# A two-dimensional spectral filter beside a token MLP: the second transform split by two instead of by four, with the combining step moved behind its matmuls

## The chip, the core and the metric

The kernel runs on one core of one Trainium2 chip. The metric is device time in microseconds (us) of one execution, median of several. Five engines work side by side, each through its own list of instructions in order: TensorE (PE in the profile; PEld are its weight loads), VectorE (DVE), ScalarE (ACT), GpSimd (POOL, nearly unused here) and SyncE (SP), which issues the DMA transfers. TensorE writes into the accumulator memory (PSUM); VectorE and ScalarE take results out of it.

## The reference

Two branches read the same x, 2048 rows (tokens) of 512 values in bf16, and a gate per row mixes them.

```python
g = sigmoid((x * gate_w).sum(-1, keepdims=True))
X = rfft2(x, axes=(-2, -1)) * (w_r + 1j * w_i)      # 2048 x 257 complex
a = irfft2(X, s=(2048, 512)).astype(bfloat16)
h = layernorm(x)
u = gelu(einsum("bsd,sf->bdf", h, w1) + b1)         # F = 1792
b = (einsum("bdf,fs->bds", u, w2) + b2).transpose(0, 2, 1)
out = g * a + (1 - g) * b
```

The first branch is a Fourier transform over rows (length 2048) and over columns (length 512), a product with a table of complex weights, and the inverse. The second is a layer norm and an MLP that mixes rows.

## The kernel before

**The MLP** is 448 accumulating matmuls' worth of 512 columns: `m1` (line 684 of the profile, 224 matmuls into 14 accumulators, gelu by ScalarE at 700) and `m2` (line 983, the same number of products, taken out by ScalarE at 989, the last two of the sixteen output tiles by VectorE at 1001). It needs nothing of the spectral branch until the very end, so its matmuls fill whatever time TensorE would wait for that branch.

**The spectral branch** is done as small transforms by matmul with radix steps by additions on VectorE between them. The names in the code, in order:

- Row index s = 512q + 4p + r. For each r (0 to 3), `q4a`/`q4b` (519 to 526) do the radix 4 over q; then `fa` (538 to 541) transforms over p by matmul. The weights (the stationary operand) of these matmuls are 128 columns of x, so the result has a column index d on the partitions: four blocks `dq` of 128 consecutive d. ScalarE evicts each into `X` (544).
- `d4a`/`d4b` (551 to 558) do the first radix 4 of the column transform, over the four blocks, on VectorE, for each r.
- `radix4(..., inverse=False)` (577 to 590) combines the four r. It runs for two halves of the frequencies, `lt` = 1 and then `lt` = 0, each as e1 (two instructions of 2048 elements per partition), e2 and e3 (two of 1024 each). The zeroth line is special: `sp0`/`sp1` (602 to 620) work on it apart, and line 628 copies it into `X` for `lt` = 0.
- `fb` (646 to 649) is the second transform: over the 128 d of a block, by matmul, for each `lt`, each of four `e` and real and imaginary part `c`: 16 groups of four matmuls. Two have 128 output columns; the other two, for the odd frequency classes, have 256 and add up in place. `fbev` (653, ScalarE) evicts each group into `B`; the accumulator holds the frequencies by class b (f = b + 4i), and the eviction reads them in turn from the four classes, so that `B` is in order of f.
- `c0a` (770, 771) copies the column of frequency 0, `nyq` (780 to 783) treats one further row, `bfly` (799, 800), `mul` (807), `comb` (812, 813), `ob` (819 to 821) form the product with the complex weights `W`, all on VectorE, first for `lt` = 0, then 1. `wprep` (756 to 760) and `c0b` prepare it.
- The inverse: `radix4(..., inverse=True)` on `B` (577, 578, 582, 583, 592, 593), whose results `T` the first inverse matmuls `i1` (868 to 875) take; evictions (881, 883), additions `zf` and `fq` (891 to 904), matmuls `i3` (942 to 946), evictions with the gate as scale (955), additions `es` (966 to 970), and the sum with the MLP (995, 1001).

**What sets the order.** The kernel is written as tasks with an engine, an estimated duration, keys that they read and write, and a priority. `Plan.order` plays them through once on a model of the engines, picks on each engine the ready task of least priority value, and the tasks are then emitted in that order. So the order on every engine is fixed when the kernel is built; on the chip an instruction that waits holds up all behind it on its engine. `fa` and `fb` groups and `i1` to `i3` take accumulators of two kinds, `fa` and `fb`, two each; `m1` and `m2` mostly use four called `acc`. A priority of 2 for `fb` against 10 and more for `m1` means: as soon as the model has the operands ready, `fb` goes first.

Of the kernel before, what the change touches and what calls it, by code (L numbers as in the profile page):

```python
# [34 lines left out]
def make_tables():  # L35
# [52 lines left out]
    tb = np.zeros((P, 3, 4, 64))  # L88
    i = np.arange(64)
    for b in (0, 2):  # L90
        th = ang(p, b + 4 * i, D)
        tb[:, 0, b // 2] = np.cos(th)
        tb[:, 1, b // 2] = -np.sin(th)
    tb[:, 1, 0, 0] = alt
    tb[:, 2, 0:2] = tb[:, 0, 0:2]
    tc = np.zeros((P, 2, 3, 2, 64))
    for n, b in enumerate((1, 3)):
        th = ang(p, b + 4 * i, D)
        sg = 1.0 if b == 1 else -1.0
# [15 lines left out]
    tb = np.concatenate([tb[:, :, 0:2].reshape(P, 384), tc.reshape(P, 768), cf.reshape(P, 8)], 1)  # L115
# [152 lines left out]
def kernel(  # L268
# [137 lines left out]
    load("tb", [P, 1160], BF16, tabs["tb"], 296960, prio=9)  # L406
# [51 lines left out]


# [3 lines left out]
    for r in range(4):  # L463
# [69 lines left out]
        for dq in range(4):  # L533
            def fa(r=r, dq=dq):
                pa = t["pa", r, dq] = ps([P, 2, 2, P], F32, "fa", 2)
                ta = t["ta"][:, r, :]
                w = lambda k: t["xf", r][:, k, dq * P:(dq + 1) * P]
                T.matmul(pa[:, 1], lhsT=w(2), rhs=ta[:, 256:512], start=True, stop=False)  # L538
                T.matmul(pa[:, 1], lhsT=w(3), rhs=ta[:, 384:640], start=False, stop=True)
                T.matmul(pa[:, 0, :, 0:64], lhsT=w(0), rhs=ta[:, 0:128], start=True, stop=True)  # L540
                T.matmul(pa[:, 0, :, 64:128], lhsT=w(1), rhs=ta[:, 128:256], start=True, stop=True)  # L541
            add("PE", mm(128, 128, 256, 256), fa, reads=[("xf", r % 2), ("ta", r)], writes=[("pa", r, dq)], prio=0, alloc=["fa"],
                free=["xf"] if dq == 3 else ())
            add("ACT", act(512), lambda r=r, dq=dq: A.copy(t["X"][:, :, r, :, dq, :], t["pa", r, dq][:]),  # L544
                reads=[("pa", r, dq)], writes=[("X", r, dq)], prio=0, free=["fa"])

        def d4a(r=r):
            xv = t["X"][:, :, r]
            s = t["st"][:, 1024:2048].rearrange("p (a c n) -> p a c n", a=2, c=2)
            two = lambda lo: xv[:, :, :, lo:lo + 2, :].rearrange("p a c j l -> p a c (j l)")  # L550
            V.tensor_add(s, two(0), two(2))
            V.tensor_sub(two(2), two(0), two(2))

        def d4b(r=r):
            xv = t["X"][:, :, r]
            s = t["st"][:, 1024:2048].rearrange("p (a c n) -> p a c n", a=2, c=2)
            V.tensor_add(xv[:, :, :, 0, :], s[:, :, :, 0:P], s[:, :, :, P:2 * P])
            V.tensor_sub(xv[:, :, :, 1, :], s[:, :, :, 0:P], s[:, :, :, P:2 * P])
        add("DVE", 2 * tt(1024), d4a, reads=[], writes=[("X", r, dq) for dq in range(4)] + ["sx"], prio=3.9)
        add("DVE", 2 * tt(512), d4b, reads=["sx"], writes=[("D", r)], prio=3.9)  # L560


    def radix4(view, pq, st, pqk, stk, reads, writes, prio, inverse):
# [16 lines left out]
        def e2():  # L580
            p, q = parts(pq)
            V.tensor_add(dst(0, 1), p, q)
            V.tensor_sub(dst(4, 1), p, q)

        def e3():
            s, u = parts(st)
            sr, ur = s[:, ::-1], u[:, ::-1]
            if not inverse:
                V.tensor_add(dst(2, 5), s, ur)
                V.tensor_sub(dst(3, 3), sr, u)  # L590
            else:
                V.tensor_add(dst(3, 3), sr, u)
                V.tensor_sub(dst(2, 5), s, ur)
# [12 lines left out]
    def sp1():  # L606
        sp, sd, fx = t["sp"], t["sd"], t["fx"]
        c = 0.5 ** 0.5
        V.tensor_add(sd[:, 0], sp[:, 0:2], sp[:, 2:4])
        V.tensor_sub(sd[:, 1], sp[:, 0:2], sp[:, 2:4])  # L610
        V.tensor_add(fx[:, 0, 0], sd[:, 0, 0, 0], sd[:, 0, 1, 0])
        V.tensor_sub(fx[:, 0, 1], sd[:, 0, 0, 0], sd[:, 0, 1, 0])
        V.tensor_copy(fx[:, 1, 0], sd[:, 1, 0, 0])
        V.tensor_scalar_mul(fx[:, 1, 1], sd[:, 1, 1, 0], -1.0)
        V.tensor_scalar_mul(sd[:, 0, 0, 1], sd[:, 1, 1, 1], c)
        V.tensor_scalar_mul(sd[:, 1, 0, 1], sd[:, 0, 1, 1], -c)
        V.tensor_add(fx[:, 2, 0], sp[:, 0, 1], sd[:, 0, 0, 1])
        V.tensor_sub(fx[:, 3, 0], sp[:, 0, 1], sd[:, 0, 0, 1])
        V.tensor_sub(fx[:, 2, 1], sd[:, 1, 0, 1], sp[:, 2, 1])
        V.tensor_add(fx[:, 3, 1], sd[:, 1, 0, 1], sp[:, 2, 1])  # L620
    add("DVE", tiny(12), sp1, reads=["sp"], writes=["fx"], prio=0)

    for lt in (1, 0):
        pr = 3.0 if lt else 3.1
# [3 lines left out]
    add("DVE", 0.15, lambda: V.tensor_copy(t["X"][:, 0, :, :, :, 0], t["fx"][:]), reads=["fx"],  # L628
        writes=[("Z", 0, 0), ("Z", 0, 1)], prio=3.1)

    def tbl(kind, c):
        tb = t["tb"]
        if kind < 2:
            return tb[:, 0:384].rearrange("p (c k i) -> p c k i", c=3, k=2)[:, c:c + 2, kind, :]
        v = tb[:, 384:1152].rearrange("p (g n) -> p g n", g=2)[:, kind - 2]
        return v[:, 128 * c:128 * c + 256]

    for lt in (0, 1):
        for e in (0, 2, 1, 3):
            for c in range(2):  # L640
                tag = ("fa", "fb")[c]

                def fb(lt=lt, e=e, c=c, tag=tag):
                    pb = t["pb", lt, e, c] = ps([P, 2, 4, 64], F32, tag, 2)
                    w = lambda k: t["X"][:, lt, e, c, k, :]
                    T.matmul(pb[:, :, 0, :], lhsT=w(0), rhs=tbl(0, c), start=True, stop=True)
                    T.matmul(pb[:, :, 2, :], lhsT=w(1), rhs=tbl(1, c), start=True, stop=True)
                    for k in (2, 3):
                        T.matmul(pb[:, :, 1::2, :], lhsT=w(k), rhs=tbl(k, c), start=(k == 2), stop=(k == 3))
                add("PE", mm(128, 128, 256, 256), fb, reads=[("Z", lt, e % 2), "tb"], writes=[("pb", lt, e, c)], prio=2, alloc=[tag])  # L650

                def fbev(lt=lt, e=e, c=c):
                    A.copy(t["B"][:, lt, e, 2 * c:2 * c + 2, :].rearrange("p s (i b) -> p s i b", b=4),  # L653
                           t["pb", lt, e, c][:].rearrange("p s b i -> p s i b"))
                add("ACT", act(512), fbev, reads=[("pb", lt, e, c)], writes=[("B", lt, e)], prio=1.8, free=[tag])
# [108 lines left out]
    for lt in range(2):  # L764
# [8 lines left out]
        if lt == 0:  # L773
# [10 lines left out]
            add("DVE", 3 * d1(512) + 0.1, nyq, reads=bk + [("W", 0), ("W", 1), ("c0", 0)] + pbk, writes=["nn"], prio=0.5)  # L784
# [261 lines left out]
```

## Time and profile before

| | |
|---|---|
| median of 3 runs | 132.45 us (132.32 to 132.88) |
| the profiled execution | 132.39 us, its span 130.5 us |
| TensorE: busy, instructions | 125.4 us, 780 matmuls |
| VectorE | 110.6 us, 248 |
| ScalarE | 83.1 us, 166 |
| DMA | 23.18 MB in 17478 packets |

The span runs from the first to the last instruction of the profiled execution; the rest of its time lies around that. Instructions are listed with their start in the span, their duration, the engine, the line of the kernel, what they write and read, and, in brackets, the idle time of the engine ahead of them and what ended it. Groups ("by line") have the count, the sum of busy time, the mean in ns, and the idle time ahead. A matmul's duration is longer than the time until the next may start, since matmuls are pipelined; the step from start to start is what it costs TensorE. Likewise the durations on VectorE and ScalarE overlap a little with the next instruction's.

### The profile page before, as it was taken

What the parts mean: (1) busy time and instruction counts of PE and PEld (TensorE: products, weight loads), DVE (VectorE), ACT (ScalarE), POOL (GpSimd) and SP (SyncE); (2) the same over time, 40 slices, a digit from 0 to 9 for tenths busy, and PEclk for the clock granted to TensorE, in tenths of its full rate; (3) what the DMA queues carried; (4) which work ended last, traced back from release to release, by engine and by line L of the source; (5) the groups of instructions that cost most, each with busy time, mean ns of one, the idle gap of its engine ahead of it and who ended that gap; (6) DMA issues with size and microseconds to landing.
All of it is one profiled execution on the core that took longest, in us unless ns stands there. A gap on an engine that the chain in (4) does not pass through costs nothing.

```text
span 130.5 us, 2166 instructions
## 1 busy us (share of the span) xinstructions
PE 125.4 (96%) x780; PEld 70.7 (54%) x780; DVE 110.6 (85%) x248; ACT 83.1 (64%) x166; POOL 0.2 (0%) x4
## 2 busy tenths in 40 slices
PE   6998999999999999999999999999999999999991
PEld 2344565545544484854444555455687577655590
DVE  2689999999999997059999999999959929999961
ACT  4468989599999999996111044322499489962200
POOL 0000000000000000000000000000000000000000
PEclk9999999999999999999999999999999999999998
DMA  4999999943669536799999800000000000312331
GB/s 83 389 372 386 398 394 379 374 91 89 135 184 298 107 85 131 259 288 406 414 421 421 334 6 0 3 5 3 0 0 0 0 5 0 161 69 97 161 121 40
DMA packets 17478, 23.18 MB, mean 178 GB/s; under 512 B 1574, under 2 KB 14908, under 8 KB 17468
## 3 DMA queue, kind: packets, MB, share of 16 engines
q1 hardware_dynamic: 17180, 22.59, 50.6%
q10 hardware_dynamic: 288, 0.46, 1.3%
q8 instruction: 6, 0.10, 0.3%
q14 instruction: 4, 0.03, 0.1%
HBM read 20.93 MB, written 2.10 MB: 176 GB/s over the span
## 4 chain that ended last, share of the span: by engine, by line
PE 58%; DVE 28%; DMA 8%; issue 2%; ACT 2%; SPq 0%; DVEq 0%
PE acc L684 18%; PE acc L983 17%; DMA wa<-in_B_w_dram 5%; PE fb L684 5%; DVE xp L807 3%; DVE st L807 3%; DMA x<-in_A_x_dram 2%; PE fa L684 2%; PE fa L538 2%; DVE xp L812 2%; DVE st L578 2%; DVE B L819 2%; DVE xp L813 2%; PE fb L868 1%; PE fa L868 1%
## 5 line engine op out<-in xcount | busy, mean ns | idle before, releaser
L983 PE MATMUL acc<-gl,wb 128*128 128x512 bf16 (+1 forms) x112 | 27.4, 373 | 0.0
L983 PE MATMUL acc<-gl,wa 128*128 128x512 bf16 (+1 forms) x112 | 27.2, 372 | 0.0
L684 PE MATMUL acc<-h,wb 128*128 128x512 bf16 x112 | 25.9, 379 | 0.0
L989 ACT ACTIVATE x<-acc,ombb,omg 128x512 bf16<-128x512 f32 x14 | 10.8, 785 | 22.7 <-PE acc L983 22.7
L983 PEld LDWEIGHTS <-wb 128*128 128x128 bf16 x126 | 13.4, 114 | 10.3 <-DMA wb<-in_B_w_dram 1.2
L983 PEld LDWEIGHTS <-wa 128*128 128x128 bf16 x126 | 13.5, 114 | 9.4
L684 PE MATMUL acc<-h,wa 128*128 128x512 bf16 x64 | 17.8, 387 | 0.6 <-DVE h L505 0.6
L684 PEld LDWEIGHTS <-wb 128*128 128x128 bf16 x112 | 10.9, 98 | 11.7
L684 PEld LDWEIGHTS <-wa 128*128 128x128 bf16 x112 | 10.4, 99 | 10.8 <-issue 2.1
L700 ACT ACTIVATE gl<-acc,b1f 128x512 bf16<-128x512 f32 x11 | 7.6, 693 | 6.8 <-PE acc L684 6.8
L478 DVE BATCH_NORM_STATS2 stats<-x 128x6 f32<-128x512 bf16 x14 | 9.4, 674 | 2.2 <-DMA x<-in_A_x_dram 2.2
L544 ACT CAST X<-fa 128x512 bf16<-128x512 f32 x16 | 9.3, 582 | 2.7 <-PE fa L541 2.5
L511 ACT ACTIVATE h<-x,nmr,rstd 128x512 bf16<-128x512 bf16 x13 | 9.8, 806 | 0.4 <-DVE nmr L502 0.2
L714 ACT ACTIVATE x<-x 128x512 bf16<-128x512 bf16 x16 | 10.1, 655 | 0.0
L684 PE MATMUL fb<-h,wa 128*128 128x512 bf16 x32 | 9.4, 379 | 0.0
L955 ACT ACTIVATE B<-fb,g 128x512 bf16<-128x512 f32 x8 | 5.9, 735 | 0.0
L955 ACT ACTIVATE B<-fa,g 128x512 bf16<-128x512 f32 x8 | 5.8, 727 | 0.0
L359 PE MATMUL fa<-xp 128*128 128x512 bf16 x10 | 4.4, 632 | 1.2 <-DVE xp L320 1.2
L684 PE MATMUL fa<-h,wa 128*128 128x512 bf16 x16 | 5.6, 379 | 0.0
L653 ACT CAST B<-fb 128x512 bf16<-128x512 f32 x8 | 5.0, 628 | 0.0
L653 ACT CAST B<-fa 128x512 bf16<-128x512 f32 x8 | 4.9, 616 | 0.0
L709 DVE TENSOR_TENSOR x<-x,gw 128x2048 bf16<-128x2048 bf16 x4 | 4.8, 1216 | 0.0
(177 smaller groups left out, 230.0 us busy)
## 6 DMA issues: line engine op xcount, KB each, us to landing
wb<-in_B_w_dram SPq DMA_DIRECT2D x11, 512.0 KB
wa<-in_B_w_dram SPq DMA_DIRECT2D x7, 512.0 KB
wa<-in_B_w_dram SPq DMA_DIRECT2D x3, 896.0 KB
x<-in_A_x_dram SPq DMA_DIRECT2D x3, 512.0 KB
wb<-in_B_w_dram SPq DMA_DIRECT2D x4, 384.0 KB
out_dram<-x SPq DMA_DIRECT2D x3, 512.0 KB
rot<-dft_ti SPq DMA_DIRECT2D x1, 736.5 KB
rot<-dft_ta SPq DMA_DIRECT2D x4, 160.0 KB
```

The source lines that it names most:

```text
L478: V.bn_stats(out=t["stats"][:, j, :], in_=t["x"][:, j // 4, j % 4, :])
L511: add("ACT", 0.71, lambda j=j: A.activation(t["h"][:, j // 4, j % 4, :], t["x"][:, j // 4, j % 4, :], ActF.Identity, bias=t["nmr"][:, j:j ...
L544: add("ACT", act(512), lambda r=r, dq=dq: A.copy(t["X"][:, :, r, :, dq, :], t["pa", r, dq][:]), reads=[("pa", r, dq)], writes=[("X", r, dq ...
L653: A.copy(t["B"][:, lt, e, 2 * c:2 * c + 2, :].rearrange("p s (i b) -> p s i b", b=4), t["pb", lt, e, c][:].rearrange("p s b i -> p s i b"))
L684: T.matmul(t["u", ft][:], lhsT=w[:, j // 4, j % 4, c * P:(c + 1) * P], rhs=t["h"][:, j // 4, j % 4, :], start=(j == jorder[0]), stop=(j == ...
L700: gelus.append(add("ACT", act(512, 1) , lambda ft=ft: A.activation(t["gl"][:, ft, :], t["u", ft][:], ActF.Gelu_apprx_tanh, bias=t["b1f"][: ...
L709: add("DVE", tt(2048), lambda r=r: V.tensor_mul(t["x"][:, :, r, :], t["x"][:, :, r, :], t["gw"][:, None, :].to_broadcast([P, 4, D])), read ...
L714: A.activation(t["x"][:, q, r, :], t["x"][:, q, r, :], ActF.Copy, accum_out=t["glog"][:, 4 * q + r:4 * q + r + 1])
L807: V.tensor_mul(o, xs, w)
L955: A.activation(t["eo", j // 2][:, j % 2], t["i3", j][:], ActF.Copy, scale=t["g"][:, j:j + 1])
L983: T.matmul(t["y", j, n][:, cs], lhsT=w[:, o, 512 * q + r:512 * q + 512:4], rhs=t["gl"][:, ft, cs], start=(ft == 0), stop=(ft == NFT - 1))
L989: A.activation(tbuf(j).rearrange("p h d -> p (h d)"), t["y", j, 0][:], ActF.Identity, bias=t["ombb2"][:, j:j + 1], scale=t["omg"][:, j:j + 1])
```

## The change

The column index is split as d = 256h + 2p + t instead of in four blocks of 128. With h and t both 0 or 1:

- `fa` takes as weights every second column of a half (a step of two elements), and its result goes into a staging area (`xe`, in `xp`) in place of `X`.
- `d2`, four additions of 512 elements per r, does a radix 2 over h and writes `X`; `d4a` and `d4b` are gone.
- `fb` is four matmuls of 128 columns, one for each t and each parity of the frequency; none accumulates. The table `tb` shrinks from 1160 to 776 columns.
- `fbev` interleaves the two parities while it reads the accumulator (one element in turn from either of two places 128 fp32 values apart) and writes back into `X`, over the weights of both `c` groups of this `e`; so it waits for both groups.
- `tb2` on VectorE does the radix 2 over t behind the matmuls, from `X` into `B`, for two `e` at once: the sum gives the lower half of the frequencies, the difference the upper half, written backwards. With the second pair of each `lt` go twice three instructions of 4 elements per partition for the columns at frequencies 0 and 128.
- The four r are laid out in another order in `X` (`EX`), and `lt` = 0 now comes ahead of `lt` = 1; the special line is copied in with `lt` = 0.

The order of the new program, as built: on TensorE the `fb` groups start at the same place in the list, the last four `fa` groups lie up to four `m1` matmuls later (the very last three), the `i1` matmuls that need the last inverse radix step (T of `lt` = 1, r = 2) have four `m2` matmuls and four of line 868 more ahead of them than before, and the `i3` matmuls eight `m2` more. On VectorE the radix 4 of `lt` = 0 comes first, the twelve small instructions of `sp1` ahead of it, then e1 and e2 of `lt` = 1, `tb2` of the first pair, e3, and the other three `tb2`, a `c0` copy among them. On ScalarE three more gate reductions (714) and a gelu stand between the last `fbev` and the tanh of the gate (716).

```diff
@@ make_tables @@
-    tb = np.zeros((P, 3, 4, 64))
...
+    tb = np.zeros((P, 2, 2, 3, 64))
+    for par in range(2):
+        for h in range(2):
+            th = ang(2 * p + h, par + 2 * np.arange(64), D)
+            tb[:, par, h, 0] = np.cos(th)
+            tb[:, par, h, 1] = -np.sin(th)
...
-    load("tb", [P, 1160], BF16, tabs["tb"], 296960, prio=9)
+    load("tb", [P, 776], BF16, tabs["tb"], 198656, prio=9)
...
+    def xe(r):
+        return t["xp"][:, 2048 * r:2048 * r + 2048].rearrange("p (a c j l) -> p a c j l", a=2, c=2, j=4)
@@ fa and its eviction @@
-                w = lambda k: t["xf", r][:, k, dq * P:(dq + 1) * P]
+                w = lambda k: t["xf", r][:, k, L * (dq // 2) + dq % 2:L * (dq // 2 + 1):2]
...
-            add("ACT", act(512), lambda r=r, dq=dq: A.copy(t["X"][:, :, r, :, dq, :], t["pa", r, dq][:]),
+            add("ACT", act(512), lambda r=r, dq=dq: A.copy(xe(r)[:, :, :, dq, :], t["pa", r, dq][:]),
...
-        def d4a(r=r):
-            V.tensor_add(s, two(0), two(2))
-            V.tensor_sub(two(2), two(0), two(2))
-        def d4b(r=r):
-            V.tensor_add(xv[:, :, :, 0, :], s[:, :, :, 0:P], s[:, :, :, P:2 * P])
-            V.tensor_sub(xv[:, :, :, 1, :], s[:, :, :, 0:P], s[:, :, :, P:2 * P])
+        def d2(r=r):
+            e, xv = xe(r), t["X"][:, :, r]
+            for i in range(2):
+                V.tensor_add(xv[:, i, :, 0:2], e[:, i, :, 0:2], e[:, i, :, 2:4])
+                V.tensor_sub(xv[:, i, :, 2:4], e[:, i, :, 0:2], e[:, i, :, 2:4])
+        add("DVE", 4 * tt(512), d2, reads=[("X", r, dq) for dq in range(4)], writes=[("D", r)], prio=3.9)
...
-    for lt in (1, 0):
+    for lt in (0, 1):
@@ second transform @@
-                    T.matmul(pb[:, :, 0, :], lhsT=w(0), rhs=tbl(0, c), start=True, stop=True)
-                    T.matmul(pb[:, :, 2, :], lhsT=w(1), rhs=tbl(1, c), start=True, stop=True)
-                    for k in (2, 3):
-                        T.matmul(pb[:, :, 1::2, :], lhsT=w(k), rhs=tbl(k, c), start=(k == 2), stop=(k == 3))
+                    pb = t["pb", lt, e, c] = ps([P, 2, 2, 2, 64], F32, tag, 2)
+                    for k in range(4):
+                        T.matmul(pb[:, k % 2, k // 2], lhsT=t["X"][:, lt, EX[e], c, k, :], rhs=tbl(k, c), start=True, stop=True)
...
-                    A.copy(t["B"][:, lt, e, 2 * c:2 * c + 2, :].rearrange("p s (i b) -> p s i b", b=4),
-                           t["pb", lt, e, c][:].rearrange("p s b i -> p s i b"))
-                add("ACT", act(512), fbev, reads=[("pb", lt, e, c)], writes=[("B", lt, e)], prio=1.8, free=[tag])
+                    A.copy(t["X"][:, lt, EX[e]].rearrange("p c j l -> p (c j l)").rearrange("p (h c g b) -> p h c g b", h=2, c=2, b=2)[:, :, c],
+                           t["pb", lt, e, c][:].rearrange("p h b s i -> p h (s i) b"))
+                add("ACT", act(512), fbev, reads=[("pb", lt, e, i) for i in range(2)], writes=[("R", lt, e, c)], prio=1.8, free=[tag])
+            if e >= 2:
+                def tb2(lt=lt, e0=e - 2):
...
+                    V.tensor_add(bh[:, :, :, 0:P], vh[:, :, 0], vh[:, :, 1])
+                    V.tensor_sub(bh[:, :, 0:4:3, L - 1:P:-1], vh[:, :, 0, 0:4:3, 1:P], vh[:, :, 1, 0:4:3, 1:P])
+                    V.tensor_sub(bh[:, :, 1:3, L - 1:P:-1], vh[:, :, 1, 1:3, 1:P], vh[:, :, 0, 1:3, 1:P])
+                    if e0:
+                        for i in range(2):
+                            bh, vh = b[:, i::2], v[:, 2 * i:2 * i + 2]
+                            V.tensor_sub(bh[:, :, 1:3, 0], vh[:, :, 0, 0:4:3, 0], vh[:, :, 1, 0:4:3, 0])
+                            V.tensor_copy(bh[:, :, 0:4:3, P], vh[:, :, 0, 1:3, 0])
+                            V.tensor_copy(bh[:, :, 1:3, P], vh[:, :, 1, 1:3, 0])
+                es_ = (e - 2, e) if e == 2 else (0, 1, 2, 3)
+                add("DVE", tt(1024) + 2 * tt(508) + tiny(6) * (e > 2), tb2, reads=[("R", lt, i, c) for i in (e - 2, e) for c in range(2)],
+                    writes=[("B", lt, i) for i in es_], prio=2.5)
```

More of the change, by code (lines that the diff above doesn't have):

```diff
@@ L582, in e2 @@
             V.tensor_add(dst(0, 1), p, q)
-            V.tensor_sub(dst(4, 1), p, q)
+            V.tensor_sub(dst(4, 1) if inverse else dst(2, 1), p, q)
         def e3():
@@ L627 @@
                dk + ([] if lt else ["sp"]), [("Z", lt, 0), ("Z", lt, 1)], pr, False)
-    add("DVE", 0.15, lambda: V.tensor_copy(t["X"][:, 0, :, :, :, 0], t["fx"][:]), reads=["fx"],
-        writes=[("Z", 0, 0), ("Z", 0, 1)], prio=3.1)
+        if lt == 0:
+            add("DVE", 0.15, lambda: V.tensor_copy(t["X"][:, 0, :, :, :, 0], t["fx"][:]), reads=["fx"],
+                writes=[("Z", 0, 0), ("Z", 0, 1)], prio=3.0)
+    EX = (0, 2, 1, 3)
     def tbl(kind, c):
[L632 to L636, printed above, removed]
+        return t["tb"][:, 192 * kind + 64 * c:192 * kind + 64 * c + P].rearrange("p (s i) -> p s i", s=2)
     for lt in (0, 1):
@@ L783, in nyq @@
                 V.tensor_mul(nn[:, :, 0], t["c0"][0:1, 0, 0, 1, :], wn[:, 0, 0:257:256])
-            add("DVE", 3 * d1(512) + 0.1, nyq, reads=bk + [("W", 0), ("W", 1), ("c0", 0)] + pbk, writes=["nn"], prio=0.5)
+            add("DVE", 3 * d1(512) + 0.1, nyq, reads=[("B", i, e) for i in range(2) for e in range(4)] + [("W", 0), ("W", 1), ("c0", 0)] + pbk, writes=["nn"], prio=0.5)
         def c0b(lt=lt):
@@ L836, in linem @@
         pl8 = t["pl8"] = ps([8, D], F32, "fa", 2)
-        T.matmul(pl8[:], lhsT=t["tb"][:, 1152:1160], rhs=t["s9"][:], start=True, stop=True)
+        T.matmul(pl8[:], lhsT=t["tb"][:, 768:776], rhs=t["s9"][:], start=True, stop=True)
     add("PE", mm(512), linem, reads=["s9", "tb"], writes=["pl8"], prio=3, alloc=["fa"], after=[combt])
```

51 lines of the change are left out of this document (17 added, 34 removed).

## The prediction

> **What bounds the kernel now.** I read the page first, then busy time by stretches, then the order of time on TensorE (PE), VectorE (DVE) and ScalarE (ACT). The page's head:
>
> ```profile
> span 130.5 us, 2166 instructions
> PE 125.4 (96%) x780; PEld 70.7 (54%) x780; DVE 110.6 (85%) x248; ACT 83.1 (64%) x166; POOL 0.2 (0%) x4
> ```
>
> Busy time alone proves no bound, since matmuls overlap. The test is the step from one matmul's start to the next, and whether it is ever longer than the matmul's columns need. In order of time on PE (start, duration):
>
> ```profile
> 45.53 0.38 PE L649 MATMUL fa<-tb,X 128*128 128x256 bf16 x2
> 45.75 0.22 PE L646 MATMUL fb<-tb,X 128*128 128x128 bf16 x1
> ...
> 94.40 0.22 PE L875 MATMUL fb<-rot,B 128*128 128x128 bf16 x1
> 94.78 0.23 PE L872 MATMUL fb<-rot,B 128*128 128x128 bf16 x1 [0.17 <-DVE B L593]
> ...
> 103.19 1.67 PE L983 MATMUL acc<-gl,wb 128*128 128x512 bf16 x7
> 104.70 0.22 PE L942 MATMUL fa<-tg,xp 128*128 128x129 bf16 x1
> ...
> 105.82 1.03 PE L983 MATMUL acc<-gl,wa 128*128 128x512 bf16 x4
> ```
>
> Two matmuls of 256 columns take 45.75 - 45.53 = 0.22 us, so 0.109 each; seven of 512 take 104.70 - 103.19 = 1.51, so 0.216 each; the twenty of about 128 columns from L942 to L946 take 105.82 - 104.70 = 1.12, so 0.056 each. PE pays for columns, and a run of twenty short ones is not held up by its weight loads. Laying these steps over the whole order of PE, I find almost no holes after 27 us: the largest is 94.40 to 94.78, where one step of 0.056 took 0.38, so 0.32 lost to L593, the last step of the inverse radix 4. The end hangs on PE too:
>
> ```profile
> 124.54 0.74 DVE L1001 SCALAR_TENSOR_TENSOR x<-acc,omg,x 128x512 bf16<-128x512 f32 x1
> ...
> 127.59 0.35 DVE L1001 SCALAR_TENSOR_TENSOR x<-fb,omg,x 128x128 bf16<-128x128 f32 x1 [0.43 <-PE fb L983]
> ```
>
> The last addition waits for the last matmul. So columns taken from PE come off the end, provided that what DVE and ACT owe to PE is not later than PE then needs it. The stretch that the change touches:
>
> ```profile
> 45.00:57.00 12.00, 12.00 (x101) 8.13 (x100) 6.44 (x13) 12.00 (x29) 0.00 (x0) 1.00 0.61 166
> ```
>
> The columns are stretch, length, then busy PE, PEld, DVE, ACT and POOL, and the granted clock, 1.00. PE and ACT are full for 12 us; DVE works 6.44 of them.
>
> **The change, part by part.**
>
> *Second transform on PE.* The 16 groups of L646 to L649 have 2 matmuls of 128 and 2 of 256 columns: 2 x 0.056 + 2 x 0.109 = 0.33. Now they are 4 of 128: 0.224. Saved 16 x 0.107 = **1.71 us**, on the path. Weights of the first transform are now read with a step of two elements (`w(k)` of `fa`). A weight load without a step (L646) and one with a step of two (L875):
>
> ```profile
> L646 PEld LDWEIGHTS <-X 128*128 128x128 bf16 x16 | 1.6, 98 | 0.4
> L875 PEld LDWEIGHTS <-B 128*128 128x128 bf16 x16 | 1.6, 98 | 0.5
> ```
>
> 98 ns either way: nothing. The table `tb` gets 98 KB shorter; PE first needs it at 45 us, long after its load: nothing.
>
> *DVE.* The steps:
>
> ```profile
> 40.22 1.22 DVE L577 TENSOR_TENSOR xp<-X 128x2048 bf16<-128x2048 bf16 x1
> ...
> 43.49 0.68 DVE L582 TENSOR_TENSOR X<-xp 128x1024 bf16<-128x1024 bf16 x1
> ...
> 45.90 1.22 DVE L577 TENSOR_TENSOR xp<-X 128x2048 bf16<-128x2048 bf16 x1
> ...
> 51.40 0.25 DVE L628 CAST X<-fx 128x32 bf16<-128x32 f32 x1
> 56.51 0.17 DVE L770 CAST c<-B 128x8 f32<-128x8 bf16 x1 [4.86 <-ACT B L653]
> ...
> 61.64 1.27 DVE L780 TENSOR_TENSOR X<-B,wn 1x512 f32<-1x512 bf16 x2
> ```
>
> The four of 1024 elements between 43.49 and 45.90 step by 0.60, which is their busy time less 0.08. The new instructions have 512 or 508 elements, the latter written backwards from an odd element, as in the `es` step:
>
> ```profile
> L968 DVE TENSOR_TENSOR es<-B 128x508 bf16<-128x508 bf16 x8 | 3.4, 420 | 0.0
> L967 DVE TENSOR_TENSOR es<-B 128x508 bf16<-128x508 bf16 x8 | 3.3, 418 | 0.0
> ...
> L970 DVE TENSOR_TENSOR B<-es 128x512 bf16<-128x512 bf16 x7 | 2.9, 418 | 0.0
> ```
>
> So 0.34 each, backwards or not. Removed: per r two of 1024 and two of 512, 2 x 0.60 + 2 x 0.34 = 1.88; added `d2`: 4 x 0.34 = 1.36. Over four r DVE gains 2.1. Added `tb2`, four times: 0.60 + 2 x 0.34 = 1.28, and twice six tiny ones at a step of 0.08 (12 such, with L577 and L578, fill 40.22 to 43.49). Together 4 x 1.28 + 1.0 = 6.1. DVE has 4 us more to do, but stood idle for 4.86 us just there. It has to be laid out in time. The last eviction of the first transform:
>
> ```profile
> 36.57 0.61 ACT L544 CAST X<-fa 128x512 bf16<-128x512 f32 x1
> ```
>
> Its matmuls come three L684 (3 x 0.216 = 0.65) later on PE, so it starts between 36.57 and 37.2. ACT has as many instructions ahead of it as before, and it was ACT that came last, so I take 36.7, and `d2` of r = 3 near 37.4 (at worst 0.5 later).
> - `d2` to 38.8; the copy of the special line and its twelve tiny ones, now ahead of the radix 4, with L577 and L578: 0.3 + 3.27, to 42.3; four of 1024: 2.4, to 44.7; the cast (L628): 45.0. PE comes to this set's first matmul at 45.42, as before: 0.4 in hand.
> - Second set: two of 2048 (1.22 less 0.08) and two of 1024, 2 x 1.14 + 2 x 0.60 = 3.5 and a hop, to 48.6. `tb2` of the first pair to 49.9, last two of radix 4 to 51.1, `tb2` with its tiny ones to 52.9, second set's pairs to 54.2 and, with a c0 copy, 56.1.
>
> *ACT.* Evictions:
>
> ```profile
> 45.95 0.59 ACT L653 CAST B<-fa 128x512 bf16<-128x512 f32 x1
> 46.43 0.59 ACT L653 CAST B<-fb 128x512 bf16<-128x512 f32 x1
> ```
>
> ```profile
> L653 ACT CAST B<-fb 128x512 bf16<-128x512 f32 x8 | 5.0, 628 | 0.0
> L653 ACT CAST B<-fa 128x512 bf16<-128x512 f32 x8 | 4.9, 616 | 0.0
> ...
> L883 ACT CAST h<-fa 128x512 bf16<-128x512 f32 x4 | 2.3, 610 | 0.0
> ```
>
> L653 already picks one element in turn from four places of the accumulator; L883 reads it straight: 616 to 628 against 610 ns. The new eviction alternates between two places 512 B apart. Bounds: 610 (L883) and 785 (L989, the dearest read of an accumulator, quoted last); I take L653's, step 0.48. Each now also waits for both halves of its pair, since it overwrites the weights of both: first start 46.1. Eight take 3.8, to 49.9; the next eight with one gelu between (0.6, an estimate between the steps of L653 and L989), to 54.3. `tb2` wants them at 48.6, 51.1, 52.9 and 54.3; they are there at 48.1, 50.0, 52.4 and 54.4. ACT is never late by more than 0.1, but only just.
>
> *Where it meets PE again.* The butterflies begin near 56.2; before, they came after the copy at 56.51 and its twin, near 57.1. Then the tanh of the gate, which the order now puts behind three more gate reductions on ACT, eats part of the lead; I put the start of L780 at 61.2 for 61.64, DVE **0.45 early** (between 0 and 0.9). From there DVE's chain to L593 is the same work, so T(1,1) is ready for PE at 94.78 - 0.45 = 94.3. PE without a wait came there at 94.40 + 0.06 = 94.46; now 1.71 earlier, but the new order puts four more L983 (0.86) and four L868 (0.44) ahead of it: 94.05. Wait 0.3, as before. Later: eight more L983 than before (1.73) stand ahead of the third transform, so its first matmul stays at 104.7. DVE's chain from there to L1001 is the same, so that L1001 stays at 124.5; behind it 0.66 for itself, then about 0.4 and 0.27 for the next two parts lead to 125.9, where PE too now lets the last one go (127.59 - 1.7). DVE and PE end level, and I take off 0.1 for that.
>
> **Sum**: -1.71 + 0.0 + 0.1 = -1.6. The profiled execution took 132.39 us (span 130.5), 0.06 under the median of 132.45: 132.39 - 1.6 = **130.8 us**.
>
> [...]
>
> **Rivals.**
>
> 1. *DVE comes later than I laid out* (hops between engines, `d2` at 37.9): 0.3 to 1.0 later at T(1,1). PE's wait there grows one for one: gain 0.6 to 1.3, so 131.1 to 131.8, middle 131.5. For it: the margins of 0.1 to 0.4. Against: each was made of steps of this trace.
> 2. *ScalarE's interleaved read is dear* (slower). Place: 46 to 54 us, where the row of stretches has ACT full. Price: up to 785 - 622 = 0.16 for each of 16, 2.6 us, all ahead of the last `tb2`, so DVE reaches T(1,1) 2.6 - 0.45 = 2.1 later than now; wait 94.78 + 2.1 - 94.05 = 2.85, 2.5 over the old: -1.71 + 2.5 = +0.8, **133.2 us**. It decides from about +0.1 us per eviction, where the gain is nothing. Against: L653, and the row of L989, which reads two operands per partition besides:
>
> ```profile
> L989 ACT ACTIVATE x<-acc,ombb,omg 128x512 bf16<-128x512 f32 x14 | 10.8, 785 | 22.7 <-PE acc L983 22.7
> ```
>
> 3. *Backward 508s at half pace.* L780, two of 512 elements in 1.27, is 0.64 each against 0.34: eight cost 2.4, DVE 1.95 late, wait 2.7: 133.0. L967 and L968 speak against it. [...]
> 4. *No gain from fewer columns*: if short matmuls were bound by their weight loads (98 ns), a group would take 4 x 0.098 = 0.39, more than 0.33: 133.3. The twenty at 0.056 speak against it.
> 5. *No wait at T(1,1) at all* (DVE 0.9 early): 0.3 more, of which DVE's own end lets through 0.1 to 0.2: 130.6, at best 130.4.
>
> **How the numbers follow.** Forecast (130.6 to 131.1) 0.60; rival 1, 0.22; rival 2, 0.07; rival 3, 0.02; rival 4, 0.02; rival 5, 0.07. Half a per cent, 0.66 us, is about what a measurement of this kernel can tell from no change (the three runs span 132.32 to 132.88). Faster by more: 0.60 + 0.07 + three quarters of rival 1, whose tail runs on past 131.8, = 0.84; within: the rest of rival 1 (0.05) and mild forms of rivals 2 and 3 (0.03), 0.08; slower: what is left of 2, 3 and 4, 0.08. The range 130.4 to 131.7 holds the same 0.84; the costs with far ends (the interleaved read, the backward writes) lie outside with their 0.08.
>
> **What would show it.** Right: 64 matmuls of 128 columns at steps of 0.056; evictions of 0.61 to 0.63 us; `tb2`'s backward writes at 0.42; the idle of 4.86 before L770 gone; first wait of PE on DVE between 94 and 94.5 and under 0.6. Wrong: evictions over 0.72, a hole on PE at the first matmul of either set or ahead of T(1,1) of more than 1 us, or a last L1001 that no longer waits for PE and starts after 126.5.

## The result, and the profile after

| | before | after |
|---|---|---|
| median of 4 runs each | 132.44 us (132.32 to 132.88) | 130.84 us (130.48 to 131.34) |
| the profiled execution, its span | 132.39, 130.5 us | 130.56, 128.8 us |
| first matmul of `fb` starts | 45.42 us | 45.57 us |
| last 1001 (now 1005) starts | 127.59 us | 125.76 us |

The time ratio is 0.9875, with a 95% interval of 0.9831 to 0.992: faster, by 1.6 us or 1.2 per cent. In a later session the changed kernel came to 0.9876 (0.9852 to 0.99). The ratios here and below leave out a few slow executions (one each in e4, e7 and e10, and some of the kernel before) and are not quotients of the medians, which hold all. Lines have moved: `m1` is 688 now, `m2` 987, `fa` 533 to 536, its eviction 539, `fb` 632, `fbev` 639, `tb2` 648 to 650 with the small ones at 654 to 656, `c0a` 774, `bfly` 803, `nyq` 784, the last inverse step 580, `i1` 872 to 879, the last sum 1005.

The page's head, with the shares of the chain that ended last:

```profile
span 128.8 us, 2178 instructions
PE 122.8 (95%) x766; PEld 69.4 (54%) x780; DVE 113.9 (88%) x272; ACT 83.2 (65%) x166; POOL 0.2 (0%) x4
...
PE 80%; DMA 14%; SPq 2%; issue 1%; DVE 0%
```

TensorE shows 2.6 us less busy time, but beside 780 weight loads the trace lists only 766 matmuls, so some records are missing; e6, whose trace has all 780, shows 123.2, so 2.2 less. VectorE gained 3.3, and the chain is TensorE's and the first loads'. The second transform on TensorE (start, duration):

```profile
45.57 0.39 PE L632 MATMUL fa<-tb,X 128*128 128x128 bf16 x4
45.80 0.39 PE L632 MATMUL fb<-tb,X 128*128 128x128 bf16 x4
46.02 0.39 PE L632 MATMUL fa<-tb,X 128*128 128x128 bf16 x4
```

A group steps by 0.22 (46.02 - 45.80), where it was 0.33. The same stretch of 12 us as shown for before (busy PE, PEld, DVE, ACT, POOL, then the clock):

```profile
45.00:57.00 12.00, 11.89 (x108) 7.62 (x109) 11.69 (x34) 12.00 (x29) 0.00 (x0) 1.00 0.68 194
```

VectorE works 11.69 of it for 6.44: its idle time there is used up. What it does, in order of time:

```profile
45.03 0.25 DVE L616 CAST X<-fx 128x32 bf16<-128x32 f32 x1
...
48.72 0.68 DVE L648 TENSOR_TENSOR B<-X 128x1024 bf16<-128x1024 bf16 x1
49.32 0.42 DVE L649 TENSOR_TENSOR B<-X 128x508 bf16<-128x508 bf16 x1
49.66 0.42 DVE L650 TENSOR_TENSOR B<-X 128x508 bf16<-128x508 bf16 x1
...
54.67 0.69 DVE L648 TENSOR_TENSOR B<-X 128x1024 bf16<-128x1024 bf16 x1 [0.25 <-ACT X L639]
...
56.38 1.22 DVE L803 TENSOR_TENSOR xp<-B 128x2048 bf16<-128x2048 bf16 x1
...
61.09 1.27 DVE L784 TENSOR_TENSOR X<-B,wn 1x512 f32<-1x512 bf16 x2
```

The last `tb2` (54.67) waited 0.25 for ScalarE; that is the only idle time of VectorE that the profile lists from 45 us until the end of the last inverse step:

```profile
93.50 0.68 DVE L580 TENSOR_TENSOR B<-st 128x1024 bf16<-128x1024 bf16 x1
```

```profile
94.04 0.22 PE L879 MATMUL fb<-rot,B 128*128 128x128 bf16 x1
94.24 0.23 PE L876 MATMUL fb<-rot,B 128*128 128x128 bf16 x1
```

Here is T(1,1), the result of the last inverse radix step: TensorE, ready at 94.04 + 0.056 = 94.10, started at 94.24, just as VectorE finished (93.50 + 0.68): a hole of 0.14, where before it was 0.32. And the end, where the last sum still waits for the last matmul:

```profile
125.10 0.34 DVE L1005 SCALAR_TENSOR_TENSOR x<-fa,omg,x 128x128 bf16<-128x128 f32 x1
125.76 0.35 DVE L1005 SCALAR_TENSOR_TENSOR x<-fb,omg,x 128x128 bf16<-128x128 f32 x1 [0.31 <-PE fb L987]
```

### The profile page after: what moved, and what is told of

It is laid out like the page before. It is cut to its first block, busy times and chain, and to the rows that moved or that the text cites. A ratio compares the mean times of both kernels' runs of the same rounds, so it can differ in the third digit from the quotient of the medians.

```text
span 128.8 us, 2178 instructions
## 1 busy us (share of the span) xinstructions
PE 122.8 (95%) x766; PEld 69.4 (54%) x780; DVE 113.9 (88%) x272; ACT 83.2 (65%) x166; POOL 0.2 (0%) x4
## 4 chain that ended last, share of the span: by engine, by line
PE 80%; DMA 14%; SPq 2%; issue 1%; DVE 0%
PE acc L987 36%; PE acc L688 24%; DMA wa<-in_B_w_dram 10%; DMA wb<-in_B_w_dram 4%; PE fb L688 3%; SPq L301 2%; PE fb L632 2%; PE fb L872 1%; PE fa L872 1%; PE fa L533 1%; PE fa L632 1%; PE fa L688 1%; PE fa L534 1%; PE fb L987 1%; PE fa L987 1%
## 5 line engine op out<-in xcount | busy, mean ns | idle before, releaser
L688 PE MATMUL acc<-h,wb 128*128 128x512 bf16 x108 | 25.3, 379 | 0.2
L688 PE MATMUL acc<-h,wa 128*128 128x512 bf16 x61 | 16.7, 379 | 0.9 <-DVE h L500 0.6
L688 PEld LDWEIGHTS <-wb 128*128 128x128 bf16 x112 | 10.7, 98 | 11.1
L688 PEld LDWEIGHTS <-wa 128*128 128x128 bf16 x112 | 10.3, 98 | 10.8 <-issue 1.9
L539 ACT CAST xp<-fa 128x512 bf16<-128x512 f32 x16 | 9.3, 580 | 2.9 <-PE fa L536 2.7
L688 PE MATMUL fb<-h,wa 128*128 128x512 bf16 x32 | 9.4, 379 | 0.0
L688 PE MATMUL fa<-h,wa 128*128 128x512 bf16 x16 | 5.6, 379 | 0.0
L639 ACT CAST X<-fb 128x512 bf16<-128x512 f32 x8 | 5.6, 696 | 0.0
L639 ACT CAST X<-fa 128x512 bf16<-128x512 f32 x8 | 5.5, 685 | 0.0
L632 PEld LDWEIGHTS <-X 128*128 128x128 bf16 x64 | 4.3, 98 | 1.7 <-issue 0.2
```

The lines of the kernel that those rows point to most:

```text
L539: add("ACT", act(512), lambda r=r, dq=dq: A.copy(xe(r)[:, :, :, dq, :], t["pa", r, dq][:]), reads=[("pa", r, dq)], writes=[("X", r, dq)], ...
L632: T.matmul(pb[:, k % 2, k // 2], lhsT=t["X"][:, lt, EX[e], c, k, :], rhs=tbl(k, c), start=True, stop=True)
L639: A.copy(t["X"][:, lt, EX[e]].rearrange("p c j l -> p (c j l)").rearrange("p (h c g b) -> p h c g b", h=2, c=2, b=2)[:, :, c], t["pb", lt, ...
L688: T.matmul(t["u", ft][:], lhsT=w[:, j // 4, j % 4, c * P:(c + 1) * P], rhs=t["h"][:, j // 4, j % 4, :], start=(j == jorder[0]), stop=(j == ...
```

## The experiments

Theory: TensorE's columns carry the gain, and it comes through whole because VectorE and ScalarE are just in time with more work; they are a second bound right behind. Rivals: the gain is that of the new order, not of the columns; or VectorE and ScalarE still have room; or VectorE has become the bound.

The start differs between executions. In twelve profiles of the changed kernel and its variants the first `fb` starts anywhere from 45.57 to 46.22 us, and the time follows. So beside the times stands a stretch that the start doesn't touch: from the first `fb` to the last line 1005 (1001), in the profiled execution. The ratio is to the kernel before, run on the same chip in the same session (medians of before 132.78, 132.94 and 132.83).

| run | median us (runs) | ratio, 95% interval | first fb | last sum | stretch |
|---|---|---|---|---|---|
| before | 132.44 (4) | | 45.42 | 127.59 | 82.17 |
| after | 130.84 (4) | 0.9875 (0.9831 to 0.992) | 45.57 | 125.76 | 80.19 |
| e12, after again | 131.17 (6) | 0.9876 (0.9852 to 0.99) | 45.91 | 126.08 | 80.17 |
| e1, columns back | 132.63 (12) | 0.9996 (0.9967 to 1.0026) | 45.71 | 127.54 | 81.83 |
| e2, more on VectorE | 132.46 (12) | 0.9985 (0.9966 to 1.0005) | 46.22 | 127.86 | 81.64 |
| e3, more on ScalarE | 132.29 (12) | 0.9968 (0.9937 to 1.0) | 46.06 | 127.48 | 81.42 |
| e4, straight read | 131.30 (6) | 0.9887 (0.9857 to 0.9916) | 46.09 | 126.81 | 80.72 |
| e5, less on TensorE | 131.32 (9) | 0.9881 (0.9841 to 0.992) | 45.70 | 125.88 | 80.18 |
| e6, less on VectorE | 130.98 (4) | 0.9837 (0.9795 to 0.9879) | 45.79 | 125.85 | 80.06 |
| e7, less on both | 131.48 (6) | 0.9838 (0.9782 to 0.9894) | 46.07 | 125.17 | 79.10 |
| e8, less after the third transform | 131.12 (4) | 0.9851 (0.9808 to 0.9894) | 46.20 | 125.96 | 79.76 |
| e9, w2 loaded first | 131.10 (6) | 0.9894 (0.9852 to 0.9936) | 45.99 | 126.65 | 80.66 |
| e10, before, w2 first | 133.06 (12) | 1.0021 (0.9987 to 1.0056) | 45.74 | 127.90 | 82.16 |
| e11, e5 and e9 together | 131.04 (6) | 0.987 (0.9842 to 0.9897) | 45.78 | 125.97 | 80.19 |

The profiles of before and e10 agree within 0.01 us in the stretch (82.17, 82.16), the two of the changed kernel within 0.02: differences of a tenth can be read there, where the times can't tell them. The times expected for e1 to e8 were worked out from the profile of the change, whose start is the earliest of the twelve, and the medians all came out higher, by 0.4 to 2.0 us; so the readings below go by the stretch, which is that of one profiled execution each.

**e1: the columns back, all else kept.**

```diff
-                    for k in range(4):
-                        T.matmul(pb[:, k % 2, k // 2], lhsT=..., rhs=tbl(k, c), start=True, stop=True)
+                    for k in range(2):
+                        T.matmul(pb[:, k], lhsT=..., rhs=t["tb"][:, 192 * k + 64 * c:192 * k + 64 * c + 256], start=True, stop=True)
+                    for k in range(2, 4):
+                        T.matmul(pb[:, k % 2, k // 2], lhsT=..., rhs=tbl(k, c), start=True, stop=True)
```

> The changed kernel with two of the four matmuls of each fb group widened from 128 to 256 columns (their second half is overwritten by the other two), so that TensorE has its 1.71 us of columns back and all else stays. Theory (TensorE's columns carry the gain): groups step by 0.33 for 0.22, the wait of 0.14 at T(1,1) goes, the last L1005 starts 1.5 to 1.7 us later than 125.76, time about 132.2. Rival (the gain comes from VectorE's and ScalarE's new order): 130.5 to 130.9, since the columns would fall into waits.

TensorE's groups in its trace, and the last sum:

```profile
45.71 0.38 PE L632 MATMUL fa<-tb,X 128*128 128x256 bf16 x2
45.92 0.28 PE L634 MATMUL fa<-tb,X 128*128 128x128 bf16 x2
46.04 0.38 PE L632 MATMUL fb<-tb,X 128*128 128x256 bf16 x2
```

```profile
127.54 0.35 DVE L1007 SCALAR_TENSOR_TENSOR x<-fb,omg,x 128x128 bf16<-128x128 f32 x1 [0.32 <-PE fb L989]
```

A group takes 46.04 - 45.71 = 0.33 again, the stretch is 81.83, 1.64 more than with the change, and the time is that of the kernel before: 0.9996. The rest of the change (`d2`, `tb2`, the eviction, the new order) is by itself worth nothing that the times show, and 0.34 us in the stretch (81.83 for 82.17); the columns carry the gain, and the rival that the new order alone does it falls. What fewer columns are worth without the new order no run shows. One part of my expectation failed: the wait at T(1,1) did not go.

```profile
95.83 0.22 PE L881 MATMUL fb<-rot,B 128*128 128x128 bf16 x1
96.03 0.23 PE L878 MATMUL fb<-rot,B 128*128 128x128 bf16 x1
```

96.03 - 95.83 - 0.056 = 0.14, as with the change. VectorE came later by the same amount: its L784 starts 17.17 us after the first `fb` (62.88 - 45.71) for 15.52 (61.09 - 45.57), since longer groups on TensorE bring the evictions later (ScalarE waits for TensorE there; the last starts at 55.44, 9.73 after the first `fb`, for 8.29), and `tb2` behind them. So the columns of this stretch are on both paths, that of TensorE and that of VectorE: T(1,1) starts 49.36 us after the first `fb` before (94.78 - 45.42), 50.32 in e1 and 48.67 with the change.

**e2 and e3: a little more on VectorE, or on ScalarE, behind the last evictions.**

```diff
@@ e2, in tb2 @@
+                    if lt == 1 and e0:
+                        V.tensor_add(bh[:, :, :, 0:P], vh[:, :, 0], vh[:, :, 1])
+                        V.tensor_add(bh[:, :, :, 0:P], vh[:, :, 0], vh[:, :, 1])
@@ e3, in fbev @@
+                    for _ in range(2 if lt == 1 and e == 3 else 1):
```

> The addition of 1024 elements in the very last tb2 is done three times (same result): VectorE has 1.2 us more at about 55 us. Theory (VectorE's lead is used up; T(1,1) comes 0.14 after TensorE): the wait of TensorE ahead of T(1,1) grows from 0.14 to 1.35, the last L1005 starts 1.2 later, time about 131.8. Rival (VectorE still has cover from its old idle time of 4.86): 130.6, no change.

> The last two evictions of the second transform (lt = 1, e = 3) are done twice (same result): ScalarE has two steps of 0.475 more. Theory (the last tb2 waits on ScalarE, 0.25 idle before it): tb2 starts at 55.6 for 54.67, wait at T(1,1) 1.1 for 0.14, time about 131.5. Rival (ScalarE has room): at most 0.2 later, 130.6 to 130.8.

In e2 the last `tb2` and what follows it on VectorE, then T(1,1) on TensorE:

```profile
55.31 0.69 DVE L648 TENSOR_TENSOR B<-X 128x1024 bf16<-128x1024 bf16 x1 [0.25 <-ACT X L639]
56.04 0.69 DVE L650 TENSOR_TENSOR B<-X 128x1024 bf16<-128x1024 bf16 x1
56.77 0.69 DVE L651 TENSOR_TENSOR B<-X 128x1024 bf16<-128x1024 bf16 x1
...
58.48 1.22 DVE L806 TENSOR_TENSOR xp<-B 128x2048 bf16<-128x2048 bf16 x1
```

```profile
95.15 0.22 PE L882 MATMUL fb<-rot,B 128*128 128x128 bf16 x1
96.34 0.23 PE L879 MATMUL fb<-rot,B 128*128 128x128 bf16 x1 [0.97 <-DVE B L580]
```

From the last `tb2` to the butterflies it is 58.48 - 55.31 = 3.17 us for 56.38 - 54.67 = 1.71: the two additions cost 1.46, not 1.2, at a step of 0.73 for 0.60. Each writes the place that the one before it wrote and starts 0.04 after its recorded end (56.04 for 55.31 + 0.69 = 56.00, 56.77 for 56.73), while the next one, L652, which writes another place, starts 0.08 ahead of that end (57.38 for 57.46); that the shared place is the cause no run shows. The stretch grew by 81.64 - 80.19 = 1.45: one for one. The wait ahead of T(1,1) is 1.13 (95.15 + 0.056 to 96.34); the rest was lost ahead of the first `i1`, which came 0.47 later behind the first `fb` (47.16 for 46.69): 0.23 on a tile of w2 (68.51 to 68.74; more on these under e4) and 0.22 just ahead of `i1` (see e11).

In e3 the last two evictions, done twice, and the `tb2` behind them:

```profile
53.87 1.38 ACT L640 CAST X<-fa 128x512 bf16<-128x512 f32 x2
55.15 1.21 ACT L640 CAST X<-fb 128x512 bf16<-128x512 f32 x2
```

```profile
56.38 0.69 DVE L649 TENSOR_TENSOR B<-X 128x1024 bf16<-128x1024 bf16 x1 [1.48 <-ACT X L640]
```

Counted from the first `fb`, `tb2` starts at 56.38 - 46.06 = 10.32 for 54.67 - 45.57 = 9.10, so 1.22 later (more than the 0.95 expected: the first pair of evictions steps by 55.15 - 53.87 = 1.28), and the stretch grew by 1.23. Neither engine has room; the rival with room to spare falls for both.

**e4: the accumulator read straight on.**

```diff
-                           t["pb", lt, e, c][:].rearrange("p h b s i -> p h (s i) b"))
+                           t["pb", lt, e, c][:].rearrange("p h b s i -> p h (b s i)"))
```

> The evictions read the accumulator straight on instead of one element in turn from two places; the frequencies then lie in another order in X, and what follows computes with them so. Theory (the interleaved read costs nothing): the sixteen still step by 0.475, tb2 starts as before, 130.6. [...]

Some of the evictions with the change, interleaved, and then of e4, straight:

```profile
46.16 0.60 ACT L639 CAST X<-fa 128x512 bf16<-128x512 f32 x1
46.62 0.62 ACT L639 CAST X<-fb 128x512 bf16<-128x512 f32 x1
...
53.38 0.76 ACT L639 CAST X<-fa 128x512 bf16<-128x512 f32 x1
53.86 0.77 ACT L639 CAST X<-fb 128x512 bf16<-128x512 f32 x1
54.34 0.83 ACT L718 ACTIVATE x<-x 128x512 bf16<-128x512 bf16 x1
```

```profile
46.67 0.60 ACT L639 CAST X<-fa 128x512 bf16<-128x512 f32 x1
47.14 0.62 ACT L639 CAST X<-fb 128x512 bf16<-128x512 f32 x1
...
53.91 0.76 ACT L639 CAST X<-fa 128x512 bf16<-128x512 f32 x1
54.38 0.77 ACT L639 CAST X<-fb 128x512 bf16<-128x512 f32 x1
```

From first to last it is 7.70 us interleaved (46.16 to 53.86) and 7.71 straight (46.67 to 54.38), and instruction by instruction the durations are the same to 0.01 (means of the eight from `fa` and the eight from `fb`: 685 and 696 ns interleaved, 682 and 694 straight). Interleaving two places of the accumulator costs ScalarE nothing that can be seen here.

The stretch is nevertheless 0.53 longer than with the change. That is not the eviction: the butterflies start 10.81 us after the first `fb` in both (56.38 - 45.57, 56.90 - 46.09). It comes later, on TensorE:

```profile
66.88 1.67 PE L987 MATMUL acc<-gl,wa 128*128 128x512 bf16 x7
69.01 0.41 PE L987 MATMUL acc<-gl,wb 128*128 128x512 bf16 x1 [0.46 <-DMA wb<-in_B_w_dram]
```

The first tile of w2 that goes into `wb` had not landed; seven steps of 0.216 after 66.88 TensorE was ready at 68.39, so 0.62 was lost (the bracket counts from the recorded end of the matmul before). In return the hole at T(1,1) is gone (95.21 to 95.26).

**e5 to e8: less work on one engine, or on both.** In e5 eight matmuls of `m1` are skipped, in e6 one `mul` is halved, e7 has both, in e8 four matmuls of `m2` are skipped.

```diff
@@ e5 and e7, m1 @@
+        if (ft, j) in [(ft, j) for ft in (12, 13) for j in jorder[4:8]]:
+            return
@@ e6 and e7, mul @@
+                if lt == 0 and comp == 1:
+                    V.tensor_mul(o[:, 4:8], xs[:, 4:8], w[:, 4:8])
+                    return
@@ e8, m2 @@
+                        if j == 14 and 4 <= ft < 8:
+                            return
```

> Eight of the 224 products of m1 are left out (four in the middle of each sum for the last two accumulators, between 53 and 62 us), 1.73 us of TensorE. Theory (after the change VectorE sets T(1,1) at 94.2): the wait ahead of T(1,1) grows from 0.14 to about 1.85, and the end moves by less than 0.2: 130.4 to 130.6. Rival (TensorE alone still sets the end): 128.9.

> One of the four products with W (lt = 0, second component) is done for half of its elements only: VectorE has about 1.1 us less at 65 us, nothing else changes. Theory (TensorE comes to T(1,1) 0.14 before VectorE): only that 0.14 goes, 130.4. Rival (VectorE now paces the kernel): 129.5.

> Both of the two former cuts together: eight products of m1 and half of one product with W left out. Theory (the two engines meet at T(1,1) and either alone holds the end): T(1,1) ready at about 93.1, TensorE there at 92.4, gain 1.1 to 1.2, 129.4 to 129.5, more than the sum of the two apart (0.2 to 0.3). Rival of TensorE alone: 128.9; of VectorE alone: as e6.

> Four of the 14 products of m2 for output tile 14 are left out, 0.86 us of TensorE behind the third transform (about 119 to 122 us). Theory (VectorE's chain from the first es to the last L1005 ends within 0.3 of TensorE's): the last L1005 starts 0.3 earlier, at 125.45, with no idle ahead of it, 130.2. Rival (TensorE alone): 0.86 earlier, 129.7.

- e5: the end did not move, 80.18 for 80.19. But the 1.73 us were lost in more than one place. By TensorE's steps 1.24 went on tiles of w2 (0.23 among the `wa` below, 1.01 ahead of `wb`) and 0.60 at T(1,1) (93.72 to 94.37); together 1.84, against 1.73 saved and 0.14 that was there:

```profile
64.77 1.93 PE L991 MATMUL acc<-gl,wa 128*128 128x512 bf16 x7
67.52 0.41 PE L991 MATMUL acc<-gl,wb 128*128 128x512 bf16 x1 [0.82 <-DMA wb<-in_B_w_dram]
```

- e6: the stretch shrank by 0.13, which is the hole of 0.14 at T(1,1); VectorE's other 0.9 us bought nothing. VectorE does not pace the kernel by itself.
- e7: 79.10, so 1.09 less, where the two apart gave 0.01 and 0.13. Either engine holds the end alone. This rests on the one profile; by its median e7 is no faster than the change. (Its times lie in two groups, 129.97 and 130.11, 131.33 to 131.77, and one at 133.96; the profile is of the first group, in which the tile of w2 had landed. The second may be those in which it had not; there is no trace of them.)
- e8: 0.43 less for 0.86 us of TensorE, and VectorE goes from the first `es` to the end without a listed wait:

```profile
125.70 0.34 DVE L1007 SCALAR_TENSOR_TENSOR x<-fa,omg,x 128x128 bf16<-128x128 f32 x1
125.96 0.34 DVE L1007 SCALAR_TENSOR_TENSOR x<-fb,omg,x 128x128 bf16<-128x128 f32 x1
```

So with the change VectorE is within 0.43 of being last at the end too.

**e9 to e11: the load of w2 out of the way.** SyncE issues `ti` (754 KB, needed at 92 us) and `tg` ahead of w2. In these runs both go behind the first eleven tiles of w2; the order of the `m2` matmuls among themselves changes a little with it, that on VectorE and ScalarE does not.

```diff
-    add("SP", 0.2, ld_ti, writes=["ti"], prio=28, nbytes=754176, ...
+    add("SP", 0.2, ld_ti, writes=["ti"], prio=60, nbytes=754176, ...
-    load("tg", [P, 642], BF16, tabs["tg"], 164352, prio=29)
+    load("tg", [P, 642], BF16, tabs["tg"], 164352, prio=61)
```

> The changed kernel once more, beside the other three. Theory: 130.5 to 131.3, with TensorE's steps from the first fb to the last L1005 at 80.2 us where the first tile of w2 for wb has landed in time, and up to 0.6 more where it has not.

> The changed kernel with the loads of ti (754 KB) and tg put behind the first eleven tiles of w2 instead of ahead of all fourteen. Theory (the change brings TensorE to the w2 tiles 1.7 us earlier, where they are only just there, and in some executions late): the first tile of wb lands about 2 us earlier, no wait on it, first fb to last L1005 at most 80.2 us, median 130.4 to 130.7, less spread than the kernel with the change. Rival (the spread is only that of the start): same median as that kernel.

> The kernel before with the same reordering of loads (ti and tg behind the first tiles of w2). Theory (before, TensorE comes to the tiles 1.7 us later and does not wait for them): no change, 132.4 to 132.8. Rival (earlier w2 helps in itself): over 0.5 us faster.

> Eight products of m1 left out as in the run before, and ti and tg loaded behind the first tiles of w2. Theory (VectorE sets T(1,1)): no wait on the load of wb now, all 1.7 us saved are lost in the wait at T(1,1), which is 1.7 to 1.9; first fb to last L1005 80.1 to 80.2, as with the change alone. Rival (only the load held the end in the run without this reordering): 79.0 or less, time 129.3.

e11 settles what e5 left open. No wait for a tile of w2 is left in it, and the saved time is lost in two waits, at the first `i1` matmuls that follow L991 (0.70, from 90.75 to 91.45) and at T(1,1):

```profile
89.43 0.67 SPq L301 DMA_DIRECT2D B<-s  x1
...
91.45 0.22 PE L880 MATMUL fa<-rot,B 128*128 128x129 bf16 x1 [0.54 <-issue]
```

```profile
93.22 0.22 PE L883 MATMUL fb<-rot,B 128*128 128x128 bf16 x1
94.46 0.23 PE L880 MATMUL fb<-rot,B 128*128 128x128 bf16 x1 [1.02 <-DVE B L580]
```

0.70 + (94.46 - 93.22 - 0.056 = 1.18) = 1.88, against 1.73 saved and 0.14 that was there: all of it. Only the second is plainly a wait for VectorE. For the first the profile names no releaser ("issue"). By the times it is a small transfer behind VectorE: SyncE issues the special line into `B` at 89.43, just after VectorE has ended the last inverse step of `lt` = 0 (88.68 + 0.68 = 89.36), the trace has its last landing at 91.36, and TensorE starts at 91.45, 2.02 us after the issue; in e2 and e3, where it waits there too, 2.07 and 2.06 later. I had expected it all at T(1,1); the sum fits, the place only partly. The stretch is 80.19, that of the change to the hundredth.

e9 failed as an improvement: 131.10 beside 131.17 for the changed kernel itself. In its profile the loads came no earlier, and a tile of w2 is still waited for:

```profile
52.80 3.45 SPq L301 DMA_DIRECT2D wa<-in_B_w_dram  x7
56.61 2.70 SPq L301 DMA_DIRECT2D wb<-in_B_w_dram  x4
```

```profile
69.17 0.41 PE L987 MATMUL acc<-gl,wb 128*128 128x512 bf16 x1 [0.28 <-DMA wb<-in_B_w_dram]
```

With the change alone SyncE issued `wa` at 51.72, in e4 at 52.93, here at 52.80 although `ti` and `tg` no longer stood ahead: SyncE was still busy with the small loads of `W`, the last of which ended at 52.2 here and at 50.2 in the profile of the change. That is 2.0 us, while `ti` and `tg` take 0.9 (50.80 to 51.72): they were the smaller part. In e12 the load was in time and the stretch 80.17, yet its profiled execution took 0.57 more than that of the change (131.13 for 130.56): 0.34 of it lie ahead of the first `fb`, and the rest outside the stretch as well.

e10 shows no gain before the change (133.06, where 132.4 to 132.8 was expected). It shows something that I had not expected: in the profile of before TensorE did lose 0.12 us on a tile of w2 (69.99 and four steps make 70.85; the next starts at 70.98). In e10 this hole is gone, but the wait at T(1,1) is 0.49 for 0.32, and the stretch is the same. So before the change too VectorE set T(1,1), and hid the late tile.

## Why the prediction was right

It forecast 130.8 us; the median is 130.84, the profiled execution 130.56 against a sum of 132.39 - 1.6.

- **TensorE, -1.71.** Right: a group steps by 0.22, and e1 gives the columns back for 1.64 in the stretch (the 0.07 that is missing was not traced).
- **Weights with a step, nothing.** Right: 98 ns for L533, as before. Rival 4 (short matmuls held up by weight loads) falls with the 0.22.
- **VectorE's layout.** Right to two tenths: the cast of the special line at 45.03 (forecast 45.0), the butterflies at 56.38 (56.2), L784 at 61.09 (61.2), T(1,1) ready at 94.2 (94.3). Rival 1 did not happen; e2 shows that it would have cost one for one, as it said.
- **Backward writes at 0.34.** Right: 49.66 - 49.32 = 0.34, and 0.42 as duration. Rival 3 falls.
- **ScalarE, step 0.48.** Right in the step (0.475) and in the end (54.34; forecast 54.3), wrong in a sign that it named: "evictions over 0.72" would show it wrong, and the last four are. The durations grow from 0.60 to 0.77 while the step stays, in e4 without interleaving as well. Rival 2 had its mechanism right (e3: one for one) and its price wrong: nothing in place of 0.16.
- **T(1,1): wait 0.3, no gain.** 0.14, so 0.18 gained: TensorE came at 94.10 (forecast 94.05), VectorE at 94.2. That TensorE came so near the forecast is in part luck. It was late by 0.15 at the first `fb` (below) and lost 0.18 ahead of the first L872 (93.26 to 93.44, by the times just after ScalarE's first eviction L887, which starts at 92.80 and takes 0.59 where e11 lists it alone, as L891); I had neither. Against that, holes of the kernel before are gone, among them the 0.12 on the tile of w2.
- **DVE and PE end level, +0.1.** Not so in the profile: the last sum waits 0.31 for TensorE. I had VectorE's chain behind the third transform as before, but it came half a microsecond earlier (first `es` at 106.37 for 106.87, the sum put at 124.5 at 124.05): on ScalarE an eviction of `m2` (L989 at 104.90) no longer stands ahead of the first one that it needs (105.07 for 105.58). e8 shows how near it was.
- **First matmul of the second transform at 45.42 as before.** It was 45.57. The new order puts three L688 between two `fa` groups of the last r, where it had four:

```profile
32.72 0.81 PE L688 MATMUL acc<-h,wa 128*128 128x512 bf16 x3
33.56 0.27 PE L533 MATMUL fa<-rot,gl 128*128 128x256 bf16 x1
```

```profile
32.92 0.59 ACT L539 CAST xp<-fa 128x512 bf16<-128x512 f32 x1 [0.29 <-PE fa L536]
```

Three steps end at 32.72 + 0.65 = 33.37, and `fa` starts at 33.56, just after ScalarE has evicted the group before (32.92 + 0.59 = 33.51): a hole of 0.19 that I had not seen; all twelve profiles with the change have it. That the eviction frees the accumulator that is waited for is read from the times; no run took it away.

Together: 0.15 - 1.71 - 0.18 = -1.74, of the -1.83 by which the last sum moved; the other 0.09 were not traced. Against the sum of -1.6 the profiled execution is 0.2 better: the 0.1 at the end that did not come, 0.18 at T(1,1) and those 0.09, less the 0.15 of the hole. The median hides this, since the first `fb` starts later in all other profiles (45.91 in e12) than in this one; that it meets the forecast to 0.04 is in part luck.

Counted at T(1,1) the sum closes, and says more. T(1,1) came 0.54 earlier (94.24 for 94.78), and from there to the last sum it is 31.52 us for 32.81, 1.29 less; 0.54 + 1.29 = 1.83. The 1.29 are the four `m2` matmuls and four of the first inverse transform that the new order puts ahead of T(1,1), 1.30 by the prediction's steps. So T(1,1) itself came earlier by only about a third of the 1.71; the rest of the saving is room ahead of it, taken by work that used to lie behind.

What I did not have at all is the load of w2. Before, TensorE came to its tiles at 68.02, now at 66.36, and they are only just there: on time in the two profiles of the changed kernel, while by its steps TensorE lost 0.23 on them in e2, 0.62 in e4, 1.24 in e5 and 0.45 in e9. How often the changed kernel itself runs into it is open.

## What to carry to other kernels

A saving on the bounding engine comes through only as far as the second engine comes earlier where the two meet, or as work from behind that place can be put ahead of it (here 0.54 and 1.29 us). So lay the second engine out in time, to the tenth, before counting the saving; here its idle time was used up almost exactly, and afterwards neither engine alone had anything left to give (0.01 and 0.13 us apart, 1.09 together). Look also at what a faster engine reaches sooner: a load may be only just in time, or already late behind another wait. When the start of a program varies from run to run, compare a stretch between two events of the trace instead of the whole time.

## What the runs showed of the hardware

- On ScalarE, sixteen evictions almost without idle between them step by 0.475 us throughout, while the recorded duration of one climbs from 0.60 to 0.77. In e1, where there are gaps between them, it stays at 0.57 to 0.62; the sixteen of the first transform (L539 with the change), with 2.9 us of idle time ahead of them in all, have a mean of 0.58. Here the duration is not the cost; the step is.
- Repeating an instruction onto the same output cost more here than its step: 0.73 for 0.60 on VectorE (1024 elements), and on ScalarE 55.15 - 53.87 = 1.28 for a pair of evictions, against 2 x 0.475. So the doubled operation overstated itself here by 0.13 on VectorE and by 0.33 on ScalarE (1.28 - 0.95).
- Where TensorE, by the times, waited for a transfer of 8 KB, it went on 2.02 to 2.07 us after the transfer's issue (e11, e2, e3).
